# A planner's model of the shared way of VectorE and GpSimd: from shared speed to whole operations in turn, with its leads and buffers set anew

## The chip, the cores and the metric

The kernel runs on one core of a Trainium2 chip. The metric is device time in microseconds, the median of several executions; lower is better. Engines are called as in the profile: PE (TensorE), DVE (VectorE), ACT (ScalarE), POOL (GpSimd), and SP, whose queue issues the transfers.

## The reference

Causal attention over 4 batches, 12 heads, 448 rows and 64 columns a head, then a block on the joined heads (768 columns): a two-dimensional Fourier transform, a normalisation and an MLP. All is float32.

```python
scores = where(mask, -1e9, q @ k.T / 8)
attn = exp(scores - max); attn = attn / (sum(attn) + 1e-9)
x = (attn @ v) joined over heads            # (4, 448, 768)
u = x + real(fft(fft(x, axis=1), axis=2))
un = (u - mean(u)) / sqrt(var(u) + 1e-6)
out = u + maximum(un @ w_ch1, 0) @ w_ch2    # 768 -> 3072 -> 768
```

## The kernel before

**Precision.** PE multiplies in fp32r. Each float32 operand is therefore split in a high part (a rounded copy, on ACT or DVE) and a low part (a subtraction, on GpSimd or DVE), and a product takes three matmuls: high by high, high by low, low by high. This is why the other engines have so much to do. The weights go through five operations first (`weights`, L742 to L764), which make floats out of their 64-bit words: two passes on ACT, then three on DVE (L752, L758, L762).

**Stages.** 24 pairs of heads go through `attend`: load (`raw`, `v`), split into `qh`, `ql`, `kh`, `kl`, scores into PSUM, a row minimum on DVE (L469), an exponential on ACT (L473), a scaling by the reciprocal sum on GpSimd or ACT (L492, L494), transposes on PE (L505), copies of them to `pa` and `pg` (L335, L337), the product with `v` (L531) and copies to `xt`. When a batch has two column blocks, `fold` prepares them for the transform on GpSimd and DVE with the tiles `d`, `e`, `o`; `dft` then multiplies by the tables `cdh`, `cdl`, `csh`, `csl` (L601, L625), adds, normalises (`bn_stats` L666, `bn_aggr` L671, `rs` L675 and L676, `un` L685) and stores to DRAM.

The MLP takes two batches as a group (g = 0, 1) and walks 12 chunks of 256 hidden columns each, 24 items in all. `f1` multiplies (PE, L978), `f2` multiplies back (L1219 in group 0, L1180 in group 1), and DVE adds each product to the accumulator in SBUF (L1168). The first C_FAST = 5 chunks of group 0 form their four quarter blocks with 8 products. All later items are "fast": a scheme with 7 products on combined operands, in which ACT copies a product out of PSUM (`keep`, tile `c`, line L335 as for all copies of ACT) before PE adds the next one to the same bank, and DVE adds others to it (L1051). The weights' combinations (`combine`, L824) and splits (`split`, L811) are made by GpSimd or DVE. In group 0 the fast chunks also store their split weights (`wp`), and group 1 loads these; for the chunks below C_FAST group 1 loads the plain weights (`wf`) and combines them itself (`kept`). `mixed` makes the combinations of the MLP's input: for group 0 just ahead of its first fast chunk, for group 1 in the stretch that C_MIX = 7 names, stored to DRAM (`td`, L940) and loaded again by `refill` (L967) for group 1's start. Both take their input through the five tiles `us`, which go out in one fixed order.

**What sets the order.** Nothing is ordered by hand. Every piece of work is a unit with an engine (or a choice, as `("G", "V")`), a cost in ns, a priority and its tiles. `Plan.order` simulates the five engines: at each step it takes, of all units that could start, the one with the earliest start, and among equals the lowest priority number. A unit can start when its inputs are there, its engine is free, and a buffer is free for each new tile (`slot`). With a choice of engines it goes to the one with the lowest biased end (`BIAS`, `LATER`, `AGAIN`, `SLOW`). The resulting list is issued as it is, and on the chip each engine works through its own part in that order. The leads (SPLIT_AT, NORM_AT, TR_AT, DFT_AT, W_LEAD, F2_LAG, MIX_LEAD, FILL_LEAD) are offsets of the priorities, 1000 for a pair or an item.

In the plan, `side` marks the operations that use the way to SBUF that DVE and GpSimd share: all of GpSimd's, and those of DVE that touch no PSUM tile. Where two of them overlap, `takes` stretches both: DVE goes on at 0.42 and GpSimd at 0.72 of its speed.

```python
o = now.get("G" if e == "V" else "V") if e in now and side[e][n] else None
if o is None or end[o] <= t:
    return c
both = end[o] - t
return c / BOTH[e] if c <= both * BOTH[e] else c + both * (1 - BOTH[e])
```

Of the kernel before, what the change touches and what calls it, by code (L numbers as in the profile page):

```python
# [75 lines left out]
class Plan:  # L76
# [11 lines left out]
    def add(self, eng, cost, prio, fn, rd=(), wr=(), phase=None):  # L88
# [8 lines left out]
        self.units.append(dict(  # L97
            n=n, engs=dict(zip(eng, cost)) if many else {eng: cost}, many=many, prio=prio, fn=fn, deps=deps, phase=phase,
            new=sorted({z[:2] for z in wr if z[0] in self.bufs}, key=str)))

    def order(self):
        units = self.units
        left = [len(u["deps"]) for u in units]
        succ = [[] for _ in units]
# [81 lines left out]
        def when(n, e):
            s = slot(units[n], e)
            return None if s is None else max(free[e], ready[n][e], s)

        while len(seq) < len(units):  # L190
            best = None
            for e, cand in pool.items():
                for n in cand:
# [19 lines left out]
            u["eng"], cost = e, takes(n, e, t)  # L213
            if e in now and side[e][n]:
                x = "G" if e == "V" else "V"
                o = now[x]
                if o is not None and end[o] > t:
                    late = (min(t + cost, end[o]) - t) * (1 - BOTH[x])
                    end[o] += late
                    free[x] += late  # L220
                    for m in succ[o]:
                        for y in units[m]["engs"]:
                            ready[m][y] = max(ready[m][y], end[o] + self.LAT.get((x, y), 100))
            if e in now:
                now[e] = n if side[e][n] else None
# [39 lines left out]
def tile_kernel(ctx, tc, qk, vv, w1, w2, cc, cd, cs, out):  # L265
# [122 lines left out]
    def attend(i):  # L388
# [50 lines left out]
        for k, rows in enumerate(rows_):  # L439
# [21 lines left out]
            add("PE", 3 * mm(n) * 1.086 + (60 if tail else 110 * len(rows) + 200), p0, f, rd=[qh, ql, kh, kl, ("idb", 0), ("mkb", 0)], wr=banks, phase="A")  # L461
# [24 lines left out]
        add("V", 113, base + 1000, f, rd=[(*ri, 0)], wr=[(*ri, 1)], phase="A")  # L486
# [35 lines left out]
        for k, (rd, parts) in enumerate((  # L522
# [60 lines left out]
    def dft(b, p0, dp):  # L583
# [3 lines left out]
        def nxt():  # L587
            pr[0] += dp
            return pr[0]
        for par in range(2):  # L590
# [47 lines left out]
            for sign in range(2):  # L638
# [6 lines left out]
                for hf in range(2):  # L645
# [748 lines left out]
```

## Time and profile before

| what | before |
|---|---|
| median of 3 runs | 942.95 us (942.83 to 944.33) |
| the profiled execution: its span, which is its time | 942.7 us |
| PE busy | 903.4 us (96%) |
| DVE busy | 796.9 us (85%) |
| POOL busy | 627.6 us (67%) |
| ACT busy | 545.3 us (58%) |
| moved by DMA | 165.84 MB, 176 GB/s in the mean |

An engine's busy time is the union of its instructions; a stretch in which it waits for a semaphore is idle, but a wait inside an instruction counts as busy. Matmul ends are modelled, so a busy PE need not be at its peak.

### The profile page before, as it was taken

To read this page: it belongs to the slowest core of one execution; us is meant where nothing else is said; L and a number is where in the kernel's file an instruction comes from. 1 tells how busy PE (TensorE), PEld (TensorE's weight loads), DVE (VectorE), ACT (ScalarE), POOL (GpSimd) and SP (SyncE) were. 2 spreads that over 40 slices of the span, in tenths; PEclk is the share of its full clock that TensorE was granted. 3 is DMA by queue.
4 is the path that set the end of the run, shared out by engine and by line. 5 is a ranking of instruction groups with operands and counts; after the bars stand their busy time and mean duration, and the time that the engine had idled before them with its cause. 6 is when DMAs were issued, how large, how long until landed. Compare 5 with 4: busy or idle time off the path is not lost.

```text
span 942.7 us, 16159 instructions
## 1 busy us (share of the span) xinstructions
PE 903.4 (96%) x5636; PEld 805.8 (85%) x5636; DVE 796.9 (85%) x1330; ACT 545.3 (58%) x1300; POOL 627.6 (67%) x648
## 2 busy tenths in 40 slices
PE   7999999999799999999999988999999999999998
PEld 4667668777688999988989887998999999999998
DVE  6889999898897887999998999997788676666668
ACT  6999798988644444545454456645454453444442
POOL 4798698884642222443543337799999898887886
PEclk9999999999899999999999999999999999999999
DMA  7624624615569556758777668665123444444403
GB/s 274 220 88 170 183 77 138 164 45 180 149 210 345 171 208 224 245 196 292 277 275 256 214 217 295 210 217 174 48 68 118 129 139 136 141 145 136 149 1 117
DMA packets 67537, 165.84 MB, mean 176 GB/s; under 512 B 18976, under 2 KB 31904, under 8 KB 67360
## 3 DMA queue, kind: packets, MB, share of 16 engines
q1 hardware_dynamic: 67456, 164.82, 52.8%
q8 instruction: 44, 0.72, 0.3%
q14 instruction: 37, 0.30, 0.1%
HBM read 112.89 MB, written 54.74 MB: 178 GB/s over the span
## 4 chain that ended last, share of the span: by engine, by line
PE 60%; DVE 21%; POOL 6%; issue 6%; ACT 6%; DMA 1%; SPq 0%; POOLq 0%; DVEq 0%; ACTq 0%
PE h L978 22%; PE o L1180 16%; PE o L1219 8%; PE x L531 4%; PE pt L505 3%; PE sc L457 3%; DVE acc L1168 3%; DVE w L762 3%; DVE w L752 2%; ACT p L473 2%; DVE w L811 1%; DVE w L758 1%; DVE mn L469 1%; DVE ws L824 1%; DVE hl L1015 1%
## 5 line engine op out<-in xcount | busy, mean ns | idle before, releaser
L1168 DVE TENSOR_TENSOR acc<-o,acc 128x384 f32<-128x384 f32 x444 | 236.8, 552 | 79.9 <-PE o L1180 56.3
L1219 PE MATMUL o<-w2l,hh 128*128 128x384 f32 x336 | 113.6, 338 | 1.4 <-POOL w2l L779 1.3
L1219 PE MATMUL o<-w2h,hh 128*128 128x384 f32 x336 | 113.3, 337 | 1.6 <-DVE acc L1168 1.6
L1219 PE MATMUL o<-w2h,hl 128*128 128x384 f32 x336 | 113.1, 337 | 0.0
L779 POOL TENSOR_TENSOR w2l<-w,w2h 128x768 fp32r<-128x768 f32 x24 | 49.7, 2071 | 78.6 <-ACT w2h L775 71.6
L494 POOL TENSOR_TENSOR p<-p,ri 128x128 f32<-128x128 f32 (+3 forms) x113 | 79.1, 729 | 22.0 <-DVE ri L485 18.1
L811 POOL TENSOR_TENSOR w<-w,w 128x384 fp32r<-128x384 f32 x33 | 39.7, 1203 | 60.1 <-ACT w L335 59.1
L978 PE MATMUL h<-u11h,w 128*128 128x448 f32 x174 | 64.8, 380 | 3.4 <-ACT u11h L335 3.0
L1219 PEld LDWEIGHTS o<-w2l,hh 128*128 128x128 f32 x336 | 63.1, 188 | 4.4 <-POOL w2l L779 2.6
L1219 PEld LDWEIGHTS o<-w2h,hh 128*128 128x128 f32 x336 | 63.2, 188 | 4.2 <-DVE acc L1168 2.3
L978 PE MATMUL h<-u22h,w 128*128 128x448 f32 x174 | 63.2, 371 | 3.2 <-DVE c L1051 3.2
L1180 PE MATMUL o<-w2h,hh 128*128 128x384 f32 x288 | 65.1, 339 | 0.3 <-DVE acc L1168 0.3
L978 PE MATMUL h<-u12h,w 128*128 128x448 f32 x174 | 64.1, 370 | 0.0
L1219 PEld LDWEIGHTS o<-w2h,hl 128*128 128x128 f32 x336 | 63.2, 188 | 0.0
L978 PE MATMUL h<-u21h,w 128*128 128x448 f32 x174 | 63.0, 367 | 0.0
L1180 PE MATMUL o<-w2l,hl 128*128 128x384 f32 x288 | 62.4, 338 | 0.4 <-DVE acc L1168 0.4
L505 PE MATMUL pt<-cst,p 128*128 128x128 f32 (+1 forms) x384 | 56.9, 281 | 2.6 <-ACT p L492 1.9
L505 PEld LDWEIGHTS pt<-cst,p 128*128 128x128 f32 (+1 forms) x384 | 41.4, 139 | 16.8 <-issue 5.7
L335 ACT COPY c<-h 128x448 f32<-128x448 f32 x57 | 30.1, 529 | 44.1 <-PE h L978 40.2
L867 POOL TENSOR_TENSOR w2h<-w,w2h 128x384 fp32r<-128x384 f32 x43 | 45.8, 1065 | 14.6 <-ACT w2h L335 14.6
L473 ACT ACTIVATE p<-sc,mn 128x448 f32<-128x448 f32 (+3 forms) x96 | 50.4, 525 | 7.6 <-DVE mn L469 6.7
L1180 PEld LDWEIGHTS o<-w2h,hh 128*128 128x128 f32 x288 | 52.1, 188 | 2.6 <-DVE acc L1168 0.6
(212 smaller groups left out, 2999.7 us busy)
## 6 DMA issues: line engine op xcount, KB each, us to landing
w<-in_w_dram SPq DMA_DIRECT2D x48, 768.0 KB, 4.9
wp<-w SPq DMA_DIRECT2D x49, 384.0 KB, 3.5
w<-wp SPq DMA_DIRECT2D x49, 384.0 KB, 3.1
wf<-w SPq DMA_DIRECT2D x34, 384.0 KB, 2.9
w<-wf SPq DMA_DIRECT2D x17, 768.0 KB, 4.3
raw<-in_qk_dram SPq DMA_DIRECT2D x23, 480.0 KB, 3.8
us<-und SPq DMA_DIRECT2D x45, 224.0 KB, 4.2
v<-in_vv_dram SPq DMA_DIRECT2D x24, 256.0 KB, 2.9
```

What stands on the lines that cost most here:

```text
L335: nc.scalar.copy(out=out, in_=in_)
L473: nc.scalar.activation(out=T[pb][:, PO[rr]:PO[rr] + n], in_=T[ps][:, c0:c0 + n], func=ACTF.Exp, scale=-1.0, bias=T[mn][:, rr:rr + 1], accu ...
L494: nc.gpsimd.tensor_tensor(out=x, in0=x, in1=z.to_broadcast([128, KE[r]]), op=ALU.mult)
L505: nc.tensor.transpose(T[ps][0:m, 128 * k:128 * k + 128], T[pb][:, PO[r] + 128 * c:PO[r] + 128 * c + m], T["cst", 0][:, 0:128])
L531: nc.tensor.matmul(out=T[xps][64 * h:64 * h + 64, q0:q0 + w], lhsT=T[v][0:kk, c, h * D:(h + 1) * D], rhs=T[src][0:kk, s0 + h * sd:s0 + h * ...
L779: nc.gpsimd.tensor_tensor(out=T[wl], in0=T[w32].bitcast(F32), in1=T[wh], op=ALU.subtract)
L811: (nc.gpsimd if eng == "G" else nc.vector).tensor_tensor(out=T[z][:, 1], in0=src(), in1=T[z][:, 0], op=ALU.subtract)
L867: (nc.gpsimd if eng == "G" else nc.vector).tensor_tensor(out=T[z][:, 384:768], in0=src(), in1=T[z][:, 0:384], op=ALU.subtract)
L978: nc.tensor.matmul(out=T[ps][:, 0:S], lhsT=a[:, t], rhs=x[:, t], start=start and k == 0, stop=stop and k == 8, skip_group_check=True)
L1168: nc.vector.tensor_tensor(out=x, in0=T[ps][:, 0:384], in1=x, op=ALU.add)
L1180: nc.tensor.matmul(out=T[ps][:, 0:384], lhsT=hpart(j, h, a)[:, k * 128:k * 128 + 128], rhs=T[z][:, 384 * b:384 * b + 384], start=start and ...
L1219: nc.tensor.matmul(out=T[ps][:, 0:384], lhsT=T[a][:, m, k * 128:(k + 1) * 128], rhs=w[:, sl], start=(m == 0 and z == 0), stop=(m == 1 and ...
```

## The change

- `takes` and `BOTH` go. The plan keeps for DVE and for GpSimd the end of its last operation on the shared way (`held`), and an operation of the other one may start only at that end less `OVER` (91 ns for DVE, 42 ns for GpSimd). Costs are no longer stretched.
- Three kinds of DVE work are marked as not using the way (`port=False`): the reciprocal, `bn_stats` and `bn_aggr`.
- C_FAST goes from 5 to 6, C_MIX from 7 to 4; leads, biases and a few costs are set anew; the table loads wait for pairs 3 to 5 rather than 0 to 2, and the first weights for pair 16 rather than 8.
- Buffers: N_QK 3 to 4, N_D 1 to 2, N_W1 7 to 8, N_C 3 to 4, and N_PA (tile `pa`) 2 to 1. The space comes from a scratch for transfers of which 1024 bytes are left.

```diff
-N_RAW, N_V, N_QK, N_PT, N_W, N_W32, N_PA = 2, 2, 3, 2, 2, 2, 2
+N_RAW, N_V, N_QK, N_PT, N_W, N_W32, N_PA = 2, 2, 4, 2, 2, 2, 1
-DFT_AT, DFT_STEP = (4036, 3873, 3298, 3640), (77, 105, 133, 132)
-W_LEAD, F2_LAG = 809, 561
+DFT_AT, DFT_STEP = (4036, 3873, 3254, 3640), (102, 105, 149, 132)
+W_LEAD, F2_LAG = 900, 490
-N_P, N_XT, N_Y, N_F, N_D = 3, 1, 1, 1, 1
+N_P, N_XT, N_Y, N_F, N_D = 3, 1, 1, 1, 2
-C_FROM, W_FROM, N_WARM = 0, 8, 11
-N_W1, N_C, N_WS, C_FAST, C_MIX = 7, 3, 3, 5, 7
-MIX_LEAD, FILL_LEAD = -94, 417
+C_FROM, W_FROM, N_WARM = 3, 16, 11
+N_W1, N_C, N_WS, C_FAST, C_MIX = 8, 4, 3, 6, 4
+MIX_LEAD, FILL_LEAD = -391, 657
-AGAIN = dict(S=-1500, V=-100, G=-1000)
-NORM_AT, TR_AT = 1675, 1894
+AGAIN = dict(S=-825, V=-100, G=-1000)
+NORM_AT, TR_AT = 1645, 1867
-BOTH = dict(V=0.42, G=0.72)
-SLOW, BIAS = 1.5, dict(S=-300, V=-100, G=-500)
+OVER = dict(V=91, G=42)
+SLOW, BIAS = 1.873, dict(S=-300, V=-114, G=-500)
...
-            e: [e == "G" or e == "V" and not any(key[0] in self.banks for key in tiles_of[u["n"]]) for u in units]
+            e: [e == "G" or e == "V" and u["port"] and not any(key[0] in self.banks for key in tiles_of[u["n"]]) for u in units]
...
-        now = {"V": None, "G": None}
-
-        def takes(n, e, t):
...
+        held = {"V": 0.0, "G": 0.0}
 
         def when(n, e):
             s = slot(units[n], e)
-            return None if s is None else max(free[e], ready[n][e], s)
+            if s is None:
+                return None
+            t = max(free[e], ready[n][e], s)
+            if e in held and side[e][n]:
+                t = max(t, held["G" if e == "V" else "V"] - OVER[e])
+            return t
...
-                        mine = t + bias[e] + takes(n, e, t) * SLOW
+                        mine = t + bias[e] + u["engs"][e] * SLOW
...
-            u["eng"], cost = e, takes(n, e, t)
...
+            u["eng"], cost = e, u["engs"][e]
             free[e] = t + cost
+            if e in held and side[e][n]:
+                held[e] = free[e]
...
-                add("V", 81, nxt(), f, rd=[(*st6, 0), (*st6, 1)], wr=[mv], phase="Q")
+                add("V", 118, nxt(), f, rd=[(*st6, 0), (*st6, 1)], wr=[mv], phase="Q", port=False)
...
-                add("G", 716, pr[0], f, rd=[mv, ("eps", 0)], wr=[rs], phase="Q")
+                add("G", 785, pr[0], f, rd=[mv, ("eps", 0)], wr=[rs], phase="Q")
...
-    nc = _bacc.Bacc("TRN2", target_bir_lowering=False, num_devices=1)
+    nc = _bacc.Bacc("TRN2", target_bir_lowering=False, num_devices=1, dynamic_dma_scratch_size=1024)
```

Left out are two PE costs of attention that rise by about 0.1 us, the two other `port=False` lines, and the old code that stretched an operation already under way.

## Rows read from the trace of the kernel before

**Rows 1.** the page: the span, and busy time by engine
```profile
span 942.7 us, 16159 instructions
...
PE 903.4 (96%) x5636; PEld 805.8 (85%) x5636; DVE 796.9 (85%) x1330; ACT 545.3 (58%) x1300; POOL 627.6 (67%) x648
```

**Rows 2.** windows: length; PE, PEld, DVE, ACT, POOL busy; clock; DMA share, GB/s
```profile
0.00:240.00 240.00, 227.44 (x2042) 165.41 (x2042) 207.46 (x431) 208.48 (x646) 182.45 (x239) 1.00 0.50 155
240.00:275.00 35.00, 28.88 (x175) 26.59 (x175) 34.36 (x44) 19.94 (x38) 24.33 (x22) 0.90 0.57 170
400.00:640.00 240.00, 224.91 (x1180) 210.75 (x1178) 226.90 (x318) 122.00 (x212) 127.61 (x93) 1.00 0.71 248
```

**Rows 3.** PE's waits: waiter, what ended them, us in total, times, longest us
```profile
PE h L978 <- ACT c L335: 9.3, 7, 2.8
...
PE h L978 <- DVE c L1051: 3.2, 3, 1.7
PE h L978 <- ACT u11h L335: 3.0, 1, 3.0
```

**Rows 4.** timeline from 522 us: start, duration, engine, line, operation, [idle before]
```profile
522.71 2.09 POOL L779 TENSOR_TENSOR w2l<-w,w2h 128x768 fp32r<-128x768 f32 x1 [4.27 <-ACT w2h L775]
...
523.13 2.48 DVE L762 SCALAR_TENSOR_TENSOR w<-w,w 128x768 uint32<-128x768 uint32 x1
...
525.53 0.61 DVE L1051 TENSOR_TENSOR c<-h,c 128x448 f32<-128x448 f32 x1
...
526.20 0.47 PE L978 MATMUL h<-u22h,w 128*128 128x448 f32 x1 [1.02 <-DVE c L1051]
```

**Rows 5.** lines L762 and L1168: minimum, median and maximum ns, first and last start
```profile
L762 DVE SCALAR_TENSOR_TENSOR w<-w,w x48: 941/949/2586, 137.7 to 612.2; 128x768 uint32<-128x768 uint32 x48
...
L1168 DVE TENSOR_TENSOR acc<-o,acc x444: 539/557/561, 300.4 to 939.2; 128x384 f32<-128x384 f32 x148
```

**Rows 6.** windows (columns as in rows 2) of the stretches with a lower clock
```profile
243.56:250.38 6.82, 5.80 (x16) 5.22 (x17) 6.82 (x7) 2.82 (x6) 6.13 (x7) 0.50 0.54 152
639.50:642.91 3.41, 3.07 (x8) 2.77 (x9) 2.19 (x4) 1.27 (x3) 3.24 (x3) 0.50 0.63 204
```

**Rows 7.** timeline at 639.8 us, PE
```profile
639.84 0.74 PE L978 MATMUL h<-t2h,w 128*128 128x448 f32 x1 [2.33 <-ACT c L335]
```

**Rows 8.** the chain, a piece at 336 us: start, us, what, count
```profile
336.00 3.71 PE h L978 x18
```

**Rows 9.** windows of 25 us, columns as in rows 2
```profile
0.00:25.00 25.00, 19.41 (x137) 11.43 (x139) 16.72 (x43) 17.05 (x56) 11.35 (x20) 1.00 0.80 275
350.00:375.00 25.00, 25.00 (x134) 23.86 (x133) 20.03 (x31) 12.52 (x18) 6.66 (x5) 1.00 0.63 210
475.00:500.00 25.00, 23.46 (x123) 21.85 (x122) 23.79 (x36) 12.44 (x20) 11.84 (x7) 1.00 0.93 331
600.00:625.00 25.00, 24.32 (x128) 22.62 (x127) 25.00 (x31) 17.31 (x36) 21.45 (x16) 1.00 0.58 186
650.00:675.00 25.00, 24.46 (x131) 22.98 (x130) 21.33 (x35) 11.58 (x28) 24.99 (x25) 1.00 0.21 74
```

**Rows 10.** transfers of tile td: duration ns, first and last issue
```profile
L940 SPq DMA_DIRECT2D td<-us x12: 319/424/1493, 420.9 to 495.5; - x12
```

**Rows 11.** timeline at 105 us, tile pa
```profile
105.27 0.48 ACT L335 COPY pa<-pt 128x384 f32<-128x384 f32 x1
...
105.76 0.33 PE L531 MATMUL x<-pa,v 64*64 64x64 f32 x4
```

**Rows 12.** tile pa in the first 242 us, PE's reads
```profile
L531 PE MATMUL x<-pa,v x192: 217/403/591, 20.5 to 236.7; 128*64 128x448 f32 x96, 64*64 64x64 f32 x96
```

**Rows 13.** line L671, and the first use of the tables by tile cdh
```profile
L671 DVE BATCH_NORM_AGGREGATE mv<-st x16: 191/198/202, 94.1 to 282.3; 112x2 f32<-112x12 f32 x12, 113x2 f32<-113x12 f32 x4
...
L601 PE MATMUL ay<-cdh,fh x96: 253/261/343, 80.9 to 265.2; 128*112 128x194 f32 x24, 128*112 128x192 f32 x24, 128*111 128x194 f32 x12, 128*111 128x192 f32 x12
```

**Rows 14.** the chain of the first 240 us by line
```profile
by line: PE x L531 14.5%; PE pt L505 12.5%; PE sc L457 11.7%; ACT p L473 6.7%; DVE mn L469 4.9%; POOL p L494 3.3%; DVE un L685 3.1%; PE ay L601 3.0%; PE an L650 2.6%; issue 2.2%; PE at L695 2.2%; ACT pa L335 2.0%; PE sc L449 1.9%; DMA cst<-
```

More of the change, by code (lines that the diff above doesn't have):

```diff
@@ L86, in __init__, with add @@
         self.units, self.writers, self.uses = [], {}, {}
-    def add(self, eng, cost, prio, fn, rd=(), wr=(), phase=None):
+    def add(self, eng, cost, prio, fn, rd=(), wr=(), phase=None, port=True):
         n = len(self.units)
@@ L97, in add @@
         self.units.append(dict(
-            n=n, engs=dict(zip(eng, cost)) if many else {eng: cost}, many=many, prio=prio, fn=fn, deps=deps, phase=phase,
+            n=n, engs=dict(zip(eng, cost)) if many else {eng: cost}, many=many, prio=prio, fn=fn, deps=deps, phase=phase, port=port,
             new=sorted({z[:2] for z in wr if z[0] in self.bufs}, key=str)))
@@ L199, in order @@
                         bias = BIAS if u["phase"] in "AQ" else LATER if u["prio"] < F0 + 1000 * (NCH - 1) else AGAIN
-                        mine = t + bias[e] + takes(n, e, t) * SLOW
-                        if any(s + bias[x] + takes(n, x, s) * SLOW < mine for x, s in (
+                        mine = t + bias[e] + u["engs"][e] * SLOW
+                        if any(s is not None and s + bias[x] + u["engs"][x] * SLOW < mine for x, s in (
                                 (x, when(n, x)) for x in u["engs"] if x != e)):
@@ L212, in order @@
                 pool[x].remove(n)
-            u["eng"], cost = e, takes(n, e, t)
[L214 to L225, printed above, removed]
+            u["eng"], cost = e, u["engs"][e]
             free[e] = t + cost
+            if e in held and side[e][n]:
+                held[e] = free[e]
             fin = free[e]
@@ L460, in attend @@
             n = sum(KE[r] for r in rows)
-            add("PE", 3 * mm(n) * 1.086 + (60 if tail else 110 * len(rows) + 200), p0, f, rd=[qh, ql, kh, kl, ("idb", 0), ("mkb", 0)], wr=banks, phase="A")
+            add("PE", 3 * mm(n) * 1.086 + (65 if tail else 165 * len(rows) + 195), p0, f, rd=[qh, ql, kh, kl, ("idb", 0), ("mkb", 0)], wr=banks, phase="A")
             for y, r in enumerate(rows):
@@ L485, in f @@
             nc.vector.reciprocal(out=T[ri], in_=T[ri])
-        add("V", 113, base + 1000, f, rd=[(*ri, 0)], wr=[(*ri, 1)], phase="A")
+        add("V", 113, base + 1000, f, rd=[(*ri, 0)], wr=[(*ri, 1)], phase="A", port=False)
         for k, r in enumerate(order_):
@@ L533, in f @@
                             rhs=T[src][0:kk, s0 + h * sd:s0 + h * sd + w], start=c == 0, stop=c == 3)
-            add("PE", mm(sum(z[2] for z in parts), 4) + 21 * len(parts) + 105 * (k == 2), base + TR_AT + 700 + 250 * k, f,
+            add("PE", mm(sum(z[2] for z in parts), 4) + 21 * len(parts) + (95, 100, 175)[k], base + TR_AT + 700 + 250 * k, f,
                 rd=[v, *rd, *([(*xps, k - 1)] if k else [])], wr=[(*xps, k)], phase="A")
@@ L666, in f @@
                         nc.vector.bn_stats(out=T[st6][0:w, hf], in_=T[u][0:w, hf * 384:(hf + 1) * 384])
-                    add("V", dve(384), pr[0] + 3, f, rd=[(*u, hf)], wr=[(*st6, hf)], phase="Q")
+                    add("V", dve(384), pr[0] + 3, f, rd=[(*u, hf)], wr=[(*st6, hf)], phase="Q", port=False)
                 ua = [(*u, hf) for hf in range(2)]
```

6 lines of the change are left out of this document (removed).

## The prediction

> **What bounds the kernel now.** I read the page first, then the stages, then PE's waits, then one stretch of the timeline. PE is busy 903.4 of 942.7 us [rows 1]: what there is to win is the 39 us in which it is not, and whatever its busy time hides. Three stages hold 34 of them [rows 2]: the first 240 us (attention and most of the four transforms) leave PE idle 12.6 us, the change-over to the MLP 6.1 of 35, and the last chunks of group 0, from 400 to 640 us, 15.1. The rest, plain chunks and group 1, runs at PE's pace.
>
> Who ends PE's waits? [rows 3] Mostly ACT's copy of a product out of PSUM (9.3 us) and DVE's sum behind it (3.2). Yet ACT is only half busy from 400 to 640 us, while DVE has 226.9 of 240 [rows 2], so the question is what DVE does. The timeline at 522 us answers [rows 4]. GpSimd starts a subtraction of 2.09 us at 522.71. DVE starts a merge of weight bits (L762) at 523.13 and is 2.48 us in it, though that operation takes 0.95 at the median [rows 5]. It ends at 525.61, 0.81 after GpSimd's end at 524.80: until about then it did nothing. The sum L1051, which reads PSUM, stands behind it in DVE's queue until 525.53, and PE waits 1.02 us for it. An operation with a PSUM operand is not held up: L1168 takes 539 to 561 ns in all 444 cases [rows 5]. So two operations of these engines that touch only SBUF run in turn. The old plan, which lets both go on at 0.42 and 0.72 of their speed, is wrong in kind: it believed L762 cheap there, and saw no reason to let L1051 go first.
>
> **The change, part by part.**
>
> *The hold.* The new plan starts such an operation only once the other engine's is within 91 or 42 ns of its end. Nothing of this reaches the chip but the order and the engine of each operation. In [rows 4] it would put L762 at about 524.7 and so would see L1051, ready earlier, in front of it. Bounds for 400 to 640 us: nothing of the 15.1 comes back, or all of it, and with it the slow clock that follows the last wait: after PE waited 2.33 us [rows 7] it was granted 0.50, the 1.2 GHz level, for 3.41 us, and worked 3.07 of them [rows 6], which is 1.5 us of lost work. I take 60% of the 15.1, since the stall of [rows 4] is what the new model sees, but a wait that ends with ACT's copy need not come from DVE: **-9.0**. Late next is then ACT's copy itself, behind casts in ACT's own order.
> The hand-over: L762 ended 0.81 us after GpSimd's recorded end and takes 0.95 alone, so it began about 0.14 ahead of that end, near the change's 91 ns.
> [...]
>
> *C_FAST 5 to 6.* Chunk 5 of group 0 goes back from 7 products to 8: 9 matmuls more, at 3.71/18 = 0.206 us [rows 8], on PE's own path: **+1.9**. Four recombinations and three splits of its weights and three copies of products leave the crowded stretch. In group 1 this chunk's weights are combined again rather than loaded, 11 operations more of the shared way, as its neighbours do at 650 to 675 us, where GpSimd is busy 24.99 of 25 and PE still 24.46 [rows 9]: one more such chunk costs that 0.54, **+0.5** (bounds 0 and 2.3, the longest wait there is near that place [rows 7]). Seven stores and seven loads of 384 KB go, two stores of 384 KB and a load of 768 KB come.
>
> *C_MIX 7 to 4, MIX_LEAD.* Twelve differences and their twelve stores `td`, now at 421 to 495 us [rows 10], move three chunks ahead, among plain chunks, where DVE has 20.03 of 25 and DMA 0.63. They leave a stretch with 23.79 and 0.93 [rows 9]. SP's queue meets the 12 slab loads and 12 stores earlier, in front of weight loads: 24 x 224 KB at 210 GB/s are 26 us of transfers in a stretch with a third of DMA free, so a weight load may come late there, to which ACT's first pass over it is exposed. With what DVE gains at 475 us this is counted in the 60%. FILL_LEAD, W_LEAD and F2_LAG only shift who goes first among ready work.
>
> *Buffers.* N_W1 8, N_C 4, N_QK 4 and N_D 2 let a producer run ahead; slower they can't make it but through order. N_PA 1 takes one away: at 105.27 ACT writes `pa` of the next pair while PE reads the old one until 106.09 [rows 11], so that copy would wait 0.8 us. Bounds: 0, or 23 x 0.8 = 18 us, were it on the path of every pair. I take 0, since a pair takes 216/23 = 9.4 us [rows 12] and PE has scores and transposes of others meanwhile. The scratch costs nothing: every transfer of this kernel is issued on SP's queue.
>
> *Costs, leads and late loads.* `bn_aggr` measures 198 ns against the plan's 81, now 118 [rows 13]: smaller errors. Table loads wait for pairs 3 to 5, the weights for pair 16; by 9.4 us a pair these are some 50 and 150 us, while the tables are first used at 80.9 [rows 13] and the MLP starts after 240: nothing for either, covered by the pairs between, and at worst a late transform, which the range of this stage has. Order, leads and costs together then act on the 12.6 us of idle PE in the first 240. 5.6 of it lie in the first 25 us [rows 9], where PE waits for the first data and which stay; of the other 7 I take 2: **-2.0** (bounds 0 and -7; more is a rival), since ACT, with 208.5 of 240 [rows 2], is as full as DVE and moves under no new model.
>
> *Change-over.* PE waits 3.0 us for `u11h` [rows 3] and more behind it, 6.1 in all [rows 2], and is then granted 0.50 for 6.82 us, busy 5.80 of them [rows 6]: 2.9 us of lost work. Of these 9.0 I take a third, **-3.0**, since the chain from the last pair through the loads to ACT's cast stays. Bounds 0 and -9.0.
>
> **Sum:** -9.0 + 1.9 + 0.5 - 2.0 - 3.0 = -11.6 against the execution's 942.7, which is its span; the median of the runs is 942.95, 0.25 more. Hence **931**. With every bound at its best, -15.1 - 1.5 + 1.9 - 7 - 9 = -30.7, it is 912; at its worst, +1.9 + 2.3 + 18, 965.
>
> **Rivals.**
> *The shared way is full (15%).* Order can't make room: at 600 to 625 us DVE is busy 25.00 of 25 and GpSimd 21.45, at 650 to 675 GpSimd 24.99 [rows 9]. Then waits only change places and the added work stays: 942.95 + 1.9 + 0.5 = 945. Against it: part of DVE's 25.00 is waiting inside operations, as in [rows 4].
> The Trainium skill (Perfetto Trace Analysis, "Optimizing Scalar/DVE Operations") says that moving work between these two engines might not help, as they share a port; [rows 9] bear it out for single stretches only.
> *One `pa` buffer paces attention (12%), the slower side.* Its place is ACT's copy behind PE's last read of `pa`; half of the 18 us, with half of my gains less the added work, -14/2 + 2.4: 942.95 + 9 - 4.6 = 947. It decides once the copy's wait exceeds the work that PE has in hand from the next pair. For it: ACT is 87% busy [rows 2] and queues all else behind a copy. Against it: the reader can go first.
> *Attention gains much more (20%).* Lines of DVE and GpSimd make 4.9 + 3.3 + 3.1 = 11.3% of the chain in the first 240 us [rows 14], 27 us. If the true order takes out a third, that is 9 us in place of my 2: 924. Against it: ACT.
> *The forecast: 53%*, some 925 to 938.
>
> **The numbers.** A measurement tells 0.2% (1.9 us) from no change. Faster: the forecast, the third rival and a sixth of the second, 0.53 + 0.20 + 0.02 = 0.75. The first rival lies on the upper edge of no change (944.8): 0.08 same, 0.07 slower; with 0.10 of the second, 0.17 slower. The range leaves out the end of the third rival below and the worse part of the second above: 917 to 945.
>
> **Right or wrong.** Right: between 400 and 640 us PE idles about 6 us rather than 15, nearly all 48 L762 take 0.95, L978 waits for ACT's copy under 4 us in all, the clock is at 0.50 for less time, and L978 has 9 matmuls more. Wrong: PE's idle time there stays while the names of the waits change; `pa` copies wait for L531; or the moved `td` traffic shows as ACT waiting for weight loads.

## The result, and the profile after

| what | before | after |
|---|---|---|
| median | 943.64 us (942.83 to 945.46) | 918.22 us (916.28 to 918.55) |
| span of the profiled execution | 942.7 us | 916.5 us |

The ratio is 0.972 (0.969 to 0.974): about 25 us faster, where 12 were forecast. The time lies inside the range, near its lower end. In the listings after, code lines are 13 lower than before: L965 is the L978 of before, L749 the L762, L1206 and L1167 the L1219 and L1180, L322 the L335. A kernel of an experiment has the numbers of after if its planner holds, else those of before.

The page of after, to be set against [rows 1], with the chain of work by engine:

```profile
span 916.5 us, 16044 instructions
...
PE 900.6 (98%) x5645; PEld 810.1 (88%) x5645; DVE 798.1 (87%) x1498; ACT 535.4 (58%) x1268; POOL 467.2 (51%) x514
...
PE 84%; POOL 4%; DVE 4%; ACT 4%; DMA 2%; issue 1%; SPq 0%; ACTq 0%; DVEq 0%
```

PE has the 9 matmuls more (x5645 against x5636) and is idle 15.9 us instead of 39.3. GpSimd has lost 134 operations and 160 us of work; DVE has won 168 operations and hardly any busy time (798.1 us against 796.9). Windows of after, columns as in [rows 2] (the fourth is the stretch of the lower clock, the last two are used further down):

```profile
0.00:240.00 240.00, 232.21 (x2046) 169.27 (x2046) 210.03 (x484) 206.98 (x639) 139.84 (x204) 1.00 0.49 154
240.00:275.00 35.00, 32.58 (x208) 29.69 (x209) 32.65 (x64) 17.73 (x35) 11.26 (x14) 0.92 0.69 207
400.00:640.00 240.00, 238.35 (x1274) 228.67 (x1273) 222.01 (x380) 135.52 (x245) 88.21 (x71) 1.00 0.68 235
238.10:245.00 6.90, 4.36 (x14) 3.09 (x15) 5.61 (x12) 2.86 (x6) 1.44 (x2) 0.57 0.88 259
384.20:579.70 195.50, 194.51 (x1040) 186.61 (x1039) 180.92 (x315) 109.35 (x182) 38.66 (x24) 1.00 0.70 248
600.00:760.00 160.00, 159.19 (x848) 152.79 (x847) 138.96 (x234) 79.46 (x181) 144.19 (x143) 1.00 0.36 120
```

From 400 to 640 us PE idles 1.65 us; it was 15.1 [rows 2], and about 6 was forecast. The second stretch at 0.50 [rows 6] is gone; the one at the change-over stays: 0.57 in the mean of 238.1 to 245 us, most of it at the 1.2 GHz level, around PE's waits for `u11h` and `u11l` in the next lines. The largest waits of PE, the merge L749, and two other waits in after:

```profile
PE h L965 <- ACT u11h L322: 2.8, 1, 2.8
PE h L965 <- DVE u11l L892: 2.7, 3, 2.0
...
PE h L965 <- ACT c L322: 1.4, 3, 0.7
```

```profile
L749 DVE SCALAR_TENSOR_TENSOR w<-w,w x48: 939/948/1444, 221.9 to 583.5; 128x768 uint32<-128x768 uint32 x48
```

```profile
ACT w L729 <- DMA w<-in_w_dram: 9.0, 4, 4.0
...
ACT pa L322 <- PE x L518: 2.2, 3, 1.5
```

The waits for ACT's copy `c` have fallen from 9.3 to 1.4 us, and no merge waits inside itself longer than 0.5 us (before: up to 1.6 over its median [rows 5]). The other two are waits that the prediction named as bad signs. They are there and small: ACT's waits for weight loads in both of its passes over them come to 10.7 us (13.5 in before), and PE waits for copies to `pa` 0.3 us in all.

**A better ruler than idle time.** In after, the steady items show what PE needs when nothing stalls it. Measured from the first matmul of one item's first product to that of the next (counting matmuls into `h` in order, 72 a plain item and 63 a fast one), a plain item of group 0 takes 29.4 us and a fast one 27.4; the first two fast ones together 56.4. Seven items from item 5 on thus need 56.4 + 5 x 27.4 = 193.4 us with C_FAST 5, and 29.4 + 56.4 + 4 x 27.4 = 195.4 with C_FAST 6. What a kernel takes above that floor is stall, seen or not (the floor is good to a microsecond or so: in e10 below, the first fast pair takes 55.0). Item by item, items 5 to 11:

```
before   34.5 23.8 27.9 34.6 28.2 28.3 31.1   208.4 = 193.4 + 15.0
after    29.4 33.7 22.7 27.4 27.4 27.4 27.4   195.5 = 195.4 +  0.1
```

All runs by this ruler (us; spans of the profiled runs; "5-12" runs from the start of item 5 to that of item 12; group 1 begins with item 12):

```
                          span  to 5  5-12  over floor  12-18  18-end
before                   942.7 389.7 208.4        15.0  166.2   178.4
after                    916.5 384.2 195.5         0.1  159.3   177.6
e1  hold alone           966.6 389.0 202.1         8.7  196.7   178.9
e2  hold, choice         933.5 389.2 203.2         9.8  162.8   178.3
e3  all but hold         935.3 391.1 198.0         2.6  167.6   178.7
e4  old choice           957.2 390.2 195.4         0.0  185.0   186.5
e5  C_FAST 5, C_MIX 7    928.6 384.0 205.7        12.3  161.6   177.2
e6  old buffers          930.7 391.1 199.5         4.1  162.3   177.8
e7  choice alone         954.5 402.3 207.4        14.0  166.5   178.3
e8  old leads            927.8 389.7 198.9         3.5  160.4   178.8
e9  C_FAST 5             920.7 381.1 204.2        10.8  158.2   177.2
e10 C_MIX 7              917.8 384.5 196.6         1.2  159.0   177.8
e11 N_PA 2               916.2 384.0 195.5         0.1  159.2   177.6
e12 OVER 0               932.2 392.4 197.6         2.2  160.4   181.8
e13 before, C_FAST 6     951.3 391.9 213.9        18.5  168.7   176.9
e14 before, nudged       959.9 405.9 208.7        15.3  166.9   178.3
e15 OVER 101, 52         923.7 390.7 197.4         2.0  157.8   177.8
e16 SLOW 1.5             955.4 387.1 198.3         2.9  183.2   186.9
e17 e2 with C_FAST 6     933.2 389.0 203.4         8.0  162.0   178.7
e18 after, nudged        914.9 382.6 195.5         0.1  159.2   177.6
```

Before to after, the 26.2 us are 5.5 ahead of item 5, 12.9 in items 5 to 12 (14.9 of stall less 2.0 of added floor), 6.9 in items 12 to 18 and 0.8 behind.

### The profile page after: what moved, and what is told of

Read it like the earlier page. It is cut to its first block, busy times and chain, and to the rows that moved or that the text cites. A ratio compares the mean times of both kernels' runs of the same rounds, so it can differ in the third digit from the quotient of the medians.

```text
span 916.5 us, 16044 instructions
## 1 busy us (share of the span) xinstructions
PE 900.6 (98%) x5645; PEld 810.1 (88%) x5645; DVE 798.1 (87%) x1498; ACT 535.4 (58%) x1268; POOL 467.2 (51%) x514
## 4 chain that ended last, share of the span: by engine, by line
PE 84%; POOL 4%; DVE 4%; ACT 4%; DMA 2%; issue 1%; SPq 0%; ACTq 0%; DVEq 0%
PE h L965 30%; PE o L1206 19%; PE o L1167 15%; PE sc L444 5%; PE x L518 5%; PE pt L492 4%; PE ay L588 2%; ACT p L460 1%; PE at L682 1%; PE an L637 1%; DMA w<-in_w_dram 1%; PE sc L436 1%; PE ay L612 1%; POOL hl L1095 1%; POOL hh L1095 1%
## 5 line engine op out<-in xcount | busy, mean ns | idle before, releaser
L766 POOL TENSOR_TENSOR w2l<-w,w2h 128x768 fp32r<-128x768 f32 x24 | 45.5, 1900 | 148.6 <-ACT w2h L762 128.2
L1206 PE MATMUL o<-w2l,hh 128*128 128x384 f32 x336 | 113.2, 337 | 0.4 <-POOL w2l L766 0.4
L1206 PE MATMUL o<-w2h,hl 128*128 128x384 f32 x336 | 113.0, 336 | 0.0
L1206 PE MATMUL o<-w2h,hh 128*128 128x384 f32 x336 | 113.0, 336 | 0.0
L481 POOL TENSOR_TENSOR p<-p,ri 128x128 f32<-128x128 f32 (+3 forms) x106 | 70.1, 689 | 70.5 <-DVE ri L472 39.6
L965 PE MATMUL h<-u11h,w 128*128 128x448 f32 x180 | 66.4, 371 | 2.8 <-ACT u11h L322 2.8
L965 PE MATMUL h<-u21h,w 128*128 128x448 f32 x180 | 66.1, 367 | 0.0
L965 PE MATMUL h<-u22h,w 128*128 128x448 f32 x180 | 65.7, 368 | 0.0
L1206 PEld LDWEIGHTS o<-w2l,hh 128*128 128x128 f32 x336 | 63.1, 188 | 2.9 <-POOL w2l L766 0.7
L1206 PEld LDWEIGHTS o<-w2h,hh 128*128 128x128 f32 x336 | 63.1, 188 | 2.2
L965 PE MATMUL h<-u12h,w 128*128 128x448 f32 x180 | 65.0, 367 | 0.0
L1167 PE MATMUL o<-w2h,hh 128*128 128x384 f32 x288 | 63.7, 339 | 0.0
L1167 PE MATMUL o<-w2l,hl 128*128 128x384 f32 x288 | 63.2, 338 | 0.0
L1206 PEld LDWEIGHTS o<-w2h,hl 128*128 128x128 f32 x336 | 63.2, 188 | 0.0
L460 ACT ACTIVATE p<-sc,mn 128x448 f32<-128x448 f32 (+3 forms) x96 | 50.6, 528 | 16.2 <-DVE mn L456 15.1
L322 ACT COPY c<-h 128x448 f32<-128x448 f32 x53 | 27.9, 528 | 48.1 <-PE h L965 47.2
L322 ACT CAST w<-w 128x384 fp32r<-128x384 f32 x59 | 28.9, 513 | 45.1 <-DVE w L749 36.2
L456 DVE TENSOR_REDUCE mn<-sc 128x1 f32<-128x448 f32 (+3 forms) x96 | 44.2, 461 | 11.4 <-PE sd L444 6.2
L1167 PEld LDWEIGHTS o<-w2h,hh 128*128 128x128 f32 x288 | 52.5, 188 | 1.7
```

The source lines that it names most:

```text
L322: nc.scalar.copy(out=out, in_=in_)
L456: nc.vector.tensor_reduce(out=T[mn][:, rr:rr + 1], in_=T[ps][:, c0:c0 + n], axis=AX, op=ALU.min)
L460: nc.scalar.activation(out=T[pb][:, PO[rr]:PO[rr] + n], in_=T[ps][:, c0:c0 + n], func=ACTF.Exp, scale=-1.0, bias=T[mn][:, rr:rr + 1], accu ...
L481: nc.gpsimd.tensor_tensor(out=x, in0=x, in1=z.to_broadcast([128, KE[r]]), op=ALU.mult)
L766: nc.gpsimd.tensor_tensor(out=T[wl], in0=T[w32].bitcast(F32), in1=T[wh], op=ALU.subtract)
L965: nc.tensor.matmul(out=T[ps][:, 0:S], lhsT=a[:, t], rhs=x[:, t], start=start and k == 0, stop=stop and k == 8, skip_group_check=True)
```

## The experiments

Ratios are to the kernel before; after has 0.972.

**Hold, and the choice of engine.** The theories: H, the hold's order brings the gain; L, places, leads and buffers bring it; E, new choice weights (SLOW, BIAS, AGAIN), which move work off GpSimd, bring it; X, hold and choice weights need one another.

e1, the kernel before with the hold and its port marks alone (the planner of after, every constant of before):

```diff
-BOTH = dict(V=0.42, G=0.72)
+OVER = dict(V=91, G=42)
```

> The kernel before with the new hold (and the three marks for work off the shared way) and nothing else: old leads, buffers, choice weights, C_FAST 5, C_MIX 7. Theory H (the gain is the order that the hold gives): most of the 25 us, 920 to 930 us, and PE idle from 400 to 640 us falls from 15 to under 7 us. Theory L (the gain is the new placement and leads, C_FAST, C_MIX, buffers): 938 to 946. Theory E (the gain is that work goes from GpSimd to DVE through the choice weights): 935 to 945, with GpSimd still busy over 600 us.

Measured: 968.19 us, ratio 1.023 (1.021 to 1.025), slower. In items 5 to 12 stall falls from 15.0 to 8.7, and group 1 gives it back five times over. Windows of e1 and of before, and in e1 the weight subtractions of group 1 (L854; line, engine, operation, count, busy us, mean ns) and PE's waits from 600 to 760 us:

```profile
600.00:760.00 160.00, 135.28 (x657) 125.83 (x656) 73.76 (x121) 66.87 (x148) 154.97 (x164) 0.91 0.34 114
```

```profile
600.00:760.00 160.00, 155.94 (x812) 146.58 (x811) 134.47 (x205) 82.11 (x184) 149.95 (x141) 0.99 0.41 135
```

```profile
L854 POOL TENSOR_TENSOR w2h<-w,w2h 128x384 fp32r<-128x384 f32 x48 | 48.9, 1019 | 9.3 <-ACT w2h L322 8.0 <-DVE w2h L324 1.3
L854 POOL TENSOR_TENSOR w2l<-w,w2l 128x384 fp32r<-128x384 f32 x48 | 48.0, 1017 | 2.5 <-ACT w2l L322 1.8
...
PE o L1167 <- POOL hh L1095: 12.8, 3, 5.7
PE h L965 <- ACT c L322: 9.8, 5, 4.8
```

GpSimd took all 96 of these subtractions, is busy 155 of 160 us, and PE waits for it while DVE has less than half a load. So the hold by itself is not the gain: H falls as stated, and 968 us lies above the ranges of L and E too.

e2, e1 with the choice weights as well; e7, the choice weights without the hold:

```diff
-AGAIN = dict(S=-1500, V=-100, G=-1000)
+AGAIN = dict(S=-825, V=-100, G=-1000)
-SLOW, BIAS = 1.5, dict(S=-300, V=-100, G=-500)
+SLOW, BIAS = 1.873, dict(S=-300, V=-114, G=-500)
```

> The kernel before with the hold and the new choice weights (SLOW, BIAS, AGAIN), all else old. Theory H: as with the hold alone, within 3 us, 920 to 930. Theory E: about 920, clearly (over 8 us) below the hold alone, GpSimd busy under 500 us. Theory L: 938 to 946.

> The kernel before with the new choice weights only; the old model of shared speed stays. Theory X (hold and choice weights need one another: the old model's stretching stood in for a dearer GpSimd, the hold takes it away and SLOW puts it back): within 6 us of the kernel before, GpSimd busy 500 to 600 us. Theory E (the move off GpSimd is the gain): 930 to 936, as with the hold.

Measured: e2 935.03 us, 0.988 (0.986 to 0.990); e7 955.60 us, 1.010 (1.008 to 1.013). In spans, the hold alone is 23.9 us slower (966.6 less 942.7) and the weights alone 11.8 (954.5 less 942.7); together they are 9.2 faster. Of the 11.8 of e7, 12.6 lie ahead of item 5, where a nudge does as much (below); the 23.9 of e1 lie all in group 1. e2's total lies in no range: it is 33 us below e1 with GpSimd at 453.1 us, as E said, but not at 920. e7 misses X's 6 us, with 10.7. X stands by the stages: in items 12 to 18 the hold with the old weights takes 196.7 us, with the new ones 162.8, the weights without hold 166.5, and before 166.2. In the same stretch DVE now does what it left lying; after has 51 of the 96 subtractions on it:

```profile
L854 POOL TENSOR_TENSOR w2l<-w,w2l 128x384 fp32r<-128x384 f32 x24 | 27.1, 1136 | 5.3 <-DVE w2l L324 5.0 <-ACT w2l L322 0.3
L854 POOL TENSOR_TENSOR w2h<-w,w2h 128x384 fp32r<-128x384 f32 x21 | 23.8, 1136 | 0.7
L854 DVE TENSOR_TENSOR w2l<-w,w2l 128x384 fp32r<-128x384 f32 x24 | 20.8, 866 | 0.0
L854 DVE TENSOR_TENSOR w2h<-w,w2h 128x384 fp32r<-128x384 f32 x27 | 17.6, 652 | 3.0 <-ACT w2h L322 2.6
```

e2 also tests the story of [rows 4]. Its merges L749, its window of items 5 to 12, and PE's largest wait from 380 to 640 us:

```profile
L749 DVE SCALAR_TENSOR_TENSOR w<-w,w x48: 898/948/2124, 230.7 to 606.4; 128x768 uint32<-128x768 uint32 x48
...
389.20:592.40 203.20, 194.86 (x1031) 184.25 (x1029) 186.78 (x314) 103.55 (x173) 38.51 (x26) 1.00 0.73 255
...
PE h L965 <- ACT c L322: 8.5, 8, 2.3
```

```profile
389.70:598.10 208.40, 196.31 (x1030) 184.25 (x1030) 196.87 (x283) 104.54 (x174) 92.74 (x64) 1.00 0.72 252
```

(The second fence is before.) GpSimd has shed 54 us here and DVE, with 31 operations more, is busy 10 us less, so its hidden waiting has shrunk, though one merge still took 2124 ns. Yet PE still waits 8.5 us for ACT's copy: that wait was mostly not DVE's hidden one.

e3, after with the old model of the shared way in place of the hold; e4, after with the old choice weights of e2's diff; e16, after with SLOW alone put back:

```diff
-SLOW, BIAS = 1.873, dict(S=-300, V=-114, G=-500)
+SLOW, BIAS = 1.5, dict(S=-300, V=-114, G=-500)
```

> The changed kernel with the old model of shared speed put back; new leads, buffers, C_FAST, C_MIX and choice weights stay. Theory H: 935 to 948, with DVE's long waits inside operations back and PE idle over 10 us from 400 to 640. Theory L: 918 to 925. Theory E: 920 to 930.

> The changed kernel with the old choice weights (SLOW 1.5, V -100, AGAIN S -1500), all else new. Theory H: 918 to 925. Theory L: 918 to 925. Theory E: over 930, GpSimd busy over 600 us again.

> The changed kernel with SLOW 1.5 alone (AGAIN and BIAS stay new). If SLOW is what holds work off GpSimd: 945 to 960, from item 12 to item 18 over 175 us rather than 159.3, GpSimd busy over 570 us. If it is AGAIN's price for ACT: 916 to 925, GpSimd under 500.

Measured: e3 937.38 us, 0.991 (0.989 to 0.993); e4 957.28 us, 1.012 (1.010 to 1.014); e16 958.96 us, 1.015 (1.012 to 1.018). SLOW decides, not AGAIN's figure for ACT: e4 and e16 agree with E and with the first theory of e16. e3 is within H's range, but PE idles 6.2 us from 400 to 640 there, not over 10. Window of e16, and PE's largest wait in it:

```profile
600.00:760.00 160.00, 142.22 (x718) 133.57 (x717) 69.08 (x124) 67.94 (x156) 156.94 (x173) 0.96 0.29 94
...
PE o L1167 <- POOL hh L1095: 14.8, 4, 6.2
```

It is e1 again: GpSimd full, DVE at 69. The plan's own costs say why (this is argued from the code): a 384-wide subtraction is 956 ns for GpSimd and 469 for DVE. In group 1, with the offsets -1000 and -100, SLOW 1.5 gives 434 against 603, so GpSimd wins even where it would end later; 1.873 gives 791 against 778, and DVE wins by a hair. The old model divided GpSimd's cost by 0.72 wherever DVE was at work, 956 / 0.72 x 1.5 - 1000 = 992, and so pushed work to DVE by another road; by its 0.42 it made DVE dearer wherever GpSimd was at work, which pushes the other way. Windows of items 12 to 18 in before, in e1 and in after:

```profile
598.10:764.30 166.20, 162.14 (x844) 152.49 (x844) 140.08 (x212) 86.05 (x193) 155.89 (x146) 0.99 0.40 132
```

```profile
591.10:787.80 196.70, 171.29 (x845) 159.43 (x844) 98.14 (x166) 88.13 (x194) 184.15 (x196) 0.93 0.35 116
```

```profile
579.70:739.00 159.30, 158.49 (x845) 152.14 (x844) 139.56 (x230) 84.47 (x189) 145.26 (x139) 1.00 0.38 127
```

For the same 844 or 845 matmuls GpSimd runs 146 operations in before and 196 in e1: the first push won. Take the stretching away, and SLOW must be set anew.

So the groups part. Items 12 to 18 take 166 to 169 us in all five kernels with the old model, 183 to 197 in the three with the hold and SLOW 1.5, and 158 to 163 in the twelve with both. Items 5 to 12 depend little on SLOW (over the floor: 0.0 us in e4, 2.9 in e16).

**Places, buffers, leads.** P: C_FAST and C_MIX free the crowded stretch; B: the buffers; D: the leads. P1 and P2: of the places it is C_FAST, or C_MIX. C, N: C_FAST pays under the old plan too, or not. HC, R: hold, choice and C_FAST are enough, or the rest is needed. Each from after unless said:

```diff
 e5   -N_W1, N_C, N_WS, C_FAST, C_MIX = 8, 4, 3, 6, 4
      +N_W1, N_C, N_WS, C_FAST, C_MIX = 8, 4, 3, 5, 7
 e9   +N_W1, N_C, N_WS, C_FAST, C_MIX = 8, 4, 3, 5, 4
 e10  +N_W1, N_C, N_WS, C_FAST, C_MIX = 8, 4, 3, 6, 7
 e13  from before: C_FAST 5 -> 6
 e17  from e2: C_FAST 5 -> 6
 e6   N_QK 4 -> 3, N_D 2 -> 1, N_W1 8 -> 7, N_C 4 -> 3, N_PA 1 -> 2
 e8   DFT_AT, DFT_STEP, W_LEAD, F2_LAG, MIX_LEAD, FILL_LEAD, NORM_AT, TR_AT as before
 e11  N_PA 1 -> 2
```

> The changed kernel with C_FAST 5 and C_MIX 7 again; hold, choice weights, leads and buffers stay new. Theory P (placement frees the stretch of group 0's seven-product chunks): 924 to 930, PE's waits for ACT's copy from 380 to 640 us back at 7 us or more. Theory B (the buffers do it, the fourth tile c above all): 914 to 921, since 9 matmuls fewer are 1.9 us, and that wait stays under 3 us. Theory D (the leads do it): as B.

> The changed kernel with C_FAST 5 alone; C_MIX stays 4. Theory P1 (the seven-product chunk 5 itself is what crowds group 0): 925 to 931, PE's waits for ACT's copy from 380 to 640 us at 5 us or more. Theory P2 (it was group 1's differences in the middle of group 0, C_MIX, that crowded it): 915 to 919, 9 matmuls fewer, that wait under 3 us, and this beats the changed kernel by up to 2 us.

> The changed kernel with C_MIX 7 alone; C_FAST stays 6. Theory P1: 917 to 921, PE's waits for ACT's copy from 380 to 640 us under 3 us. Theory P2: 924 to 930, that wait at 5 us or more.

Measured: e5 929.59 us, 0.984 (0.980 to 0.987); e9 922.57 us, 0.975 (0.972 to 0.979); e10 919.43 us, 0.972 (0.969 to 0.975). Putting back both places costs 10 us in items 5 to 12, C_MIX alone 1, C_FAST alone 9. e10 is as P1 said; e9 lies in neither range, and its waits for ACT's copy are 1.2 us, not P1's 5. So e9 shows that these 9 are no price of a product more or less. Its items 5 to 11 take 42.1, 23.7, 27.4, 27.4, 27.4, 27.4 and 28.7 us: the first is 8.4 us over, the last 1.3, the others within 1 of their floor. Windows of e9 over item 5 and over items 7 to 10, and PE's waits in it:

```profile
381.10:423.20 42.10, 37.36 (x184) 33.97 (x184) 37.87 (x67) 18.60 (x30) 7.69 (x4) 0.94 0.68 227
...
447.00:556.50 109.50, 109.50 (x589) 105.67 (x588) 97.44 (x171) 60.33 (x97) 23.53 (x16) 1.00 0.70 248
```

```profile
PE h L965 <- ACT u12h L322: 2.0, 1, 2.0
PE h L965 <- ACT t2h L322: 1.0, 1, 1.0
```

PE waits for combined inputs of group 0 (`u12`, `t2`), and then works for a stretch at the 1.2 GHz level (0.54 in the mean of 417.3 to 424.6 us, 0.94 in that of the item). The nearest suspect, the differences for group 1 that C_MIX 4 sends through the same five tiles `us`, is too early to hold them up directly; their stores in e9:

```profile
L927 SPq DMA_DIRECT2D td<-us x12: 319/320/937, 292.2 to 352.9; - x12
```

The last is issued 28 us ahead of item 5. What makes the inputs late there stays open. In e5 the first fast pair takes 33.8 and 22.9, no stall, and the stall sits in items 7 to 11 (31.2, 28.9, 31.6, 26.6, 30.8), beginning in the stretch in which C_MIX 7 has these differences stored (415 to 501 us).

> The kernel before with C_FAST 6 and nothing else. Theory C (a seven-product chunk of group 0 costs more time than its PE work, because the other engines can't follow; giving one back frees time even under the old plan): from the first matmul of item 5 to that of item 12 about 200 us rather than 208.4, and 934 to 940 in all. Theory N (with the old model the freed engine time is lost again; C_FAST costs its 1.9 us): 209 to 211 us there, 943 to 948 in all.

> The kernel before with the hold, the new choice weights and C_FAST 6; C_MIX, buffers and leads stay old. Theory HC (the hold and C_FAST together free the stretch): 195 to 200 us from item 5 to item 12, where the hold with C_FAST 5 took 203.2 and C_FAST 6 under the old model 213.9. Theory R (it also takes the new buffers, leads or C_MIX): 203 to 214 there. From item 12 to 18 both expect 158 to 163, as with the hold and SLOW in every run so far; the total is left open, since what lies ahead of item 5 moves by 15 us at a nudge.

Measured: e13 954.55 us, 1.010 (1.006 to 1.013); e17 935.18 us, 0.988 (0.985 to 0.991), as e2. Under the old plan C_FAST 6 alone raises items 5 to 12 by 5.5 us, 2.0 of floor and 3.5 of stall; with hold and choice it changes 203.2 to 203.4. C and HC fall. R stands; N has the direction, but the loss is larger than its range (213.9 us against 211, 954.55 against 948). PE's largest waits in e13, 391 to 606 us:

```profile
PE h L978 <- DVE c L1051: 6.4, 2, 4.0
PE h L978 <- ACT c L335: 4.4, 4, 2.0
```

The sum L1051 of [rows 4] is there, twice as long in all as before [rows 3].

> The changed kernel with the old buffers (N_QK 3, N_D 1, N_W1 7, N_C 3, N_PA 2), all else new. Theory B: 924 to 930, PE's waits for ACT's copy from 380 to 640 us at 7 us or more, the fourth tile c gone. Theories P and D: 917 to 921, that wait under 3 us.

> The changed kernel with the old leads (DFT_AT, DFT_STEP, W_LEAD, F2_LAG, MIX_LEAD, FILL_LEAD, NORM_AT, TR_AT), all else new. Theory D: 925 to 932, with the loss spread over attention and group 0. Theories P and B: 917 to 922.

> The changed kernel with two tiles pa again. If one tile paces attention (the rival of the prediction): 905 to 914, the first matmul of the MLP 4 us or more earlier than at 237.5 us. If it costs nothing: 916 to 921, that matmul within 2 us of 237.5.

Measured: e6 932.13 us, 0.986 (0.983 to 0.989); e8 929.43 us, 0.983 (0.981 to 0.985); e11 920.11 us, 0.972 (0.970 to 0.976). In items 5 to 12 the old buffers bring back 4.0 us of stall and the old leads 3.4; both also lose 5 to 7 ahead of item 5, on which more below. So P, B and D each find a loss when their part alone is put back, and none of them is the whole; the waits for ACT's copy came to 6.6 us in e5 and 5.1 in e6, short of the 7 that P and B named. One `pa` or two is the same in total; the first matmul of the MLP comes at 240.7 us in e11, 3.2 later than in after, where within 2 was expected.

**How much is chance of one order?** The list is planned, so any constant may shuffle all of it. e12 and e15 are after with other hand-over figures; e14 and e18 move the transforms' priorities by a thousandth of a pair, in before and in after:

```diff
 e12  -OVER = dict(V=91, G=42)
      +OVER = dict(V=0, G=0)
 e15  +OVER = dict(V=101, G=52)
 e14  -DFT_AT, DFT_STEP = (4036, 3873, 3298, 3640), (77, 105, 133, 132)
      +DFT_AT, DFT_STEP = (4036, 3873, 3299, 3640), (78, 106, 134, 133)
 e18  -DFT_AT, DFT_STEP = (4036, 3873, 3254, 3640), (102, 105, 149, 132)
      +DFT_AT, DFT_STEP = (4036, 3873, 3255, 3640), (103, 106, 150, 133)
```

> A control: the changed kernel with the hand-over (OVER) at 0 ns for both engines rather than 91 and 42, nothing else. If the plan's result depends smoothly on its numbers: 917 to 922. If it hangs on the exact numbers, since leads and weights were set for them: over 923, and then effects of that size in the other runs can't be put down to the edited part alone.

> A control: the changed kernel with the hand-over 10 ns earlier (OVER 101 and 52). If only a wrong hand-over hurts (the loss with 0 ns was the 91 and 42 ns that it mispriced): 916 to 921. If any other order of attention hurts, as in a set of numbers picked for this very order: 922 to 934, with most of the loss ahead of item 1 and under 4 us behind it.

> A control: the kernel before with the transforms' leads one unit later (DFT_AT[2] and all of DFT_STEP plus 1, a thousandth of a pair). If the old plan is steady: 940 to 947, the first matmul of item 1 within 2 us of 276.5. If the place of the transforms is a matter of chance: 948 to 960, with the loss ahead of item 1 and under 3 us behind it.

> A control: the changed kernel with the transforms' leads one unit later (DFT_AT[2] and all of DFT_STEP plus 1), the same nudge as was given to the kernel before. If the new plan is steadier than the old one: 916 to 921. If the place of the transforms is as much a matter of chance: 922 to 935, the loss ahead of item 5, and 195 to 200 us from item 5 to item 12 all the same.

Measured: e12 933.94 us, 0.987 (0.985 to 0.990); e15 926.33 us, 0.980 (0.978 to 0.982); e14 958.33 us, 1.015 (1.011 to 1.018); e18 915.93 us, 0.968 (0.964 to 0.971). A nudge without meaning costs the kernel before 17.2 us in its span, 16.2 of them ahead of item 5 (389.7 to 405.9), and gives after 1.6. As expected by the second theory, e12, e14 and e15 lose time, but not where it said: in e14 about half of it (8.3 us) lies ahead of item 1 and 7.9 in item 1, in e15 nearly all in items 1 and 2. e18 agrees with its first theory. Windows of 275 to 400 us in after, e14 and e15:

```profile
275.00:400.00 125.00, 125.00 (x663) 119.38 (x662) 101.12 (x157) 57.97 (x89) 31.21 (x19) 1.00 0.74 257
```

```profile
275.00:400.00 125.00, 120.29 (x653) 113.25 (x654) 101.22 (x165) 57.78 (x91) 30.61 (x26) 0.97 0.67 225
```

```profile
275.00:400.00 125.00, 122.26 (x632) 116.01 (x631) 96.35 (x147) 53.77 (x82) 30.71 (x19) 0.97 0.72 244
```

The mean clock of 0.97 is a second stretch at the 1.2 GHz level, behind waits for the first chunks' weights (PE for `w2l`: 2.4 us in each). So ahead of item 5 nothing under some 16 us can be credited to an edit by one run; behind item 5 the same four edits move items 5 to 12 by 0 to 2.1 us and items 12 to 18 by 0.1 to 1.5 (and what follows item 18 by up to 4.2, in e12). e4 and e16, which differ only in a weight for attention and one for the work from about item 11 on, are 2.9 apart in items 5 to 12. That is well below the 12.4 of e3, the 12.2 of e5 and the 6.3 of e1, but the 4.0 of the buffers and the 3.4 of the leads are not far above it, and the 2.5 that after loses without the hold (e3) is not above it.

## Why the prediction was wrong in size

The sum fell short by 14.6 us (-11.6 against -26.2 in spans). By stage, 8.2 of them are group 1 (+0.5 forecast, -7.7 measured from item 12 on), 5.8 are items 5 to 12 (-9.0 + 1.9 against -12.9; its 400 to 640 us reach a little into group 1), 0.5 the stages ahead.

**The hold, -9.0 (400 to 640 us).** This step failed twice. Its size: "60% of the 15.1", because a wait that ends with ACT's copy need not be DVE's. The bound "all of it" was right: above the floor, 14.9 of 15.0 us came back, and the slow-clock stretch behind it with them. Its cause: the whole sum was given to the hold. e1 gives the hold alone 6.3 us of stall in items 5 to 12 (15.0 to 8.7), and e3 shows all the rest without the hold bringing 12.4 (15.0 to 2.6). What took the rest away is the set: buffers 4.0, leads 3.4 and hold 2.5 when each is taken out of after, and C_FAST 6, without which 10.7 come back. Buffers, of which I wrote that "a producer run ahead" can't make it slower, and leads, which "only shift who goes first", stood at nothing in the sum for this stretch. The 2.5 to 4.0 are near what a nudge moves, and e9's 10.7 is mostly one late item of open cause, so the shares of the parts are not settled; that the hold alone gives under half, and the rest without it most, is. The doubt about ACT's copy was right all the same: e2.

**C_FAST 5 to 6, +1.9.** Right as a price of PE's time: 29.4 against 27.4 us an item is 2.0. It failed as a term of its own, since the same edit is worth +5.5 (e13), +0.2 (e17) and -8.7 us (e9 to after) in items 5 to 12, by what else is in the plan.

**Group 1, +0.5.** Wrong in sign. Items 12 to 18 fell by 6.9 us though a chunk more is combined there. The step that failed is the one that took the shared way there as fixed: the prediction looked at GpSimd's 24.99 of 25 [rows 9], and priced no choice weights at all. In before 85 of the 96 subtractions of group 1 are on GpSimd; with SLOW 1.873 and the hold, DVE takes 51 of them. Hold and weights alone bring 3.4 of the 6.9 us (e2), and without the hold 8.3 are lost again (e3). That GpSimd's load is what cost before its time there is argued: PE's one long wait in that stretch ended with ACT's copy [rows 7]. In e1 and e16, where GpSimd is fuller, PE's largest wait there ends with GpSimd's `hh`.

The Trainium skill (Perfetto Trace Analysis, "Optimizing Scalar/DVE Operations") says that moving work between these two engines might not help. Here it did help: one weight that moves it from GpSimd to DVE, SLOW, makes the difference between 958.96 us (e16) and 918.22.

**Attention -2.0 and change-over -3.0.** Measured: -5.5 ahead of item 5 (the first matmul of the MLP comes 4.0 earlier, the rest follows behind it). The sum agrees with -5.0 by luck. Windows from the start to 13.5 us ahead of that matmul, and from there to the first matmul of item 1, in before and in after:

```profile
0.00:228.00 228.00, 216.90 (x1946) 157.79 (x1946) 198.60 (x413) 198.11 (x622) 174.03 (x225) 1.00 0.49 153
228.00:276.50 48.50, 40.92 (x286) 35.61 (x285) 44.71 (x65) 30.64 (x64) 32.74 (x35) 0.93 0.61 181
```

```profile
0.00:25.00 25.00, 21.93 (x111) 13.16 (x113) 15.15 (x39) 14.52 (x49) 5.73 (x15) 1.00 0.38 127
0.00:224.00 224.00, 220.07 (x1944) 160.72 (x1945) 196.98 (x457) 192.12 (x603) 128.94 (x190) 1.00 0.45 145
224.00:272.40 48.40, 42.12 (x296) 35.83 (x295) 44.18 (x88) 31.66 (x69) 22.16 (x29) 0.93 0.76 229
```

The change-over gained 0.1 us instead of 3.0, at the same mean clock of 0.93. Attention gained 4.0 instead of 2.0; PE's idle time in the first 25 us, which the prediction took as fixed, fell from 5.6 to 3.1. The other 1.4 lie in items 1 to 4. And e12, e14 and e15 move these stages by up to 16 us without meaning anything, so none of these sizes can be credited to a step.

**The rivals.** One `pa` buffer: refuted, e11 against after (0.972 both), with ACT's waits for PE's reads 2.2 us in all. The reader does go first. The shared way is full: refuted for the change as a whole. e1, e4 and e16 come near it, with GpSimd full and a wait for it ahead of all others, but DVE is less than half busy there: it is GpSimd that is full, and the choice weights decide that. Attention gains much more: no, the added gain is behind item 5.

**The signs.** Right: PE idle (1.65, better than 6), L749 at 0.95, ACT-copy waits under 4 us, less time at the slow clock, 9 matmuls. They are all signs of less stall. None of them tells hold from buffers, which is why they came true with the wrong working.

**Settled and open.** Settled: most of the time went from stall in items 5 to 12 and from items 12 to 18; in the latter hold and SLOW need each other; `pa` costs nothing. Open, and not tried further: which of the four buffers and eight leads it is, what the new costs, the late loads and the three port marks do by themselves, what makes the first fast item late in e9, how much of the 5.5 us ahead of item 5 is chance, and the true hand-over figure, since of what e12 and e15 lose against after, 8.2 of 15.7 us and 6.5 of 7.2 lie ahead of item 5 too.

## What to carry to other kernels

Where a planner's cost model changes, weights that were tuned on the old model are part of it: price them with it, and test the model with old and new weights. Take the shortest repetition of a repeated item in the same trace as its floor and count what the others take above it; this counts stalls that idle time doesn't show, and tells where they are. Before a few microseconds are credited to an edit of a planned order, nudge a constant without meaning in both kernels and see, stage by stage, what moves.

## What the runs showed of the hardware that I had not expected

**PE's idle time hides part of each stall.** In items 5 to 12 of before PE is idle 12.1 us, yet the stretch is 15.0 above its floor. The other 2.9 lie inside busy time: a matmul of L978 is recorded with some 370 ns while 18 of them start within 3.71 us [rows 8], so the record of the last one covers the first 0.17 us of a gap. The ends of matmuls are modelled, so this is a property of the record and not of the engine. Busy time per matmul shows the same, 196.31 / 1030 = 0.191 us before and 194.51 / 1040 = 0.187 after.

**A subtraction costs DVE more where both engines work.** The 128x384 subtractions take DVE 652 and 866 ns in the mean in after (and 1195 and 930 in before), against the 469 of the plan:

```profile
L854 DVE TENSOR_TENSOR w2h<-w,w2h x27: 548/558/1446, 619.9 to 893.1; 128x384 fp32r<-128x384 f32 x27
...
L854 DVE TENSOR_TENSOR w2l<-w,w2l x24: 558/900/1385, 621.7 to 902.7; 128x384 fp32r<-128x384 f32 x24
```

The 21 of them that no GpSimd operation overlaps take 557 to 559 ns; every longer one overlaps one. The excess is recorded as busy, so even a plan that holds leaves such waiting inside operations. DVE is still the quicker place: GpSimd's take 1136 in the mean.
